# A new written order for the first two batches of a fused attention and expert kernel

## The chip, the cores and the metric

The kernel runs on one core of one Trainium2 chip. The metric is device time in microseconds. Of the kernel before there are three runs: 467.71, 467.88 and 467.96 us, median 467.88 us.

## The reference

Eight batches, eight heads, 576 positions, head size 64, and 32 packed queries a head. In float32:

```
p_packed = softmax(p k^T / 8) v          # 32 rows a head
out      = softmax(q p_packed^T / 8) p_packed
x        = out, heads side by side       # 4608 x 512
h        = max(x w1, x w2, x w3)         # 4608 x 768
result   = h w_out                       # 4608 x 512
```

## The kernel before

The kernel never forms x. Since x = a p_packed with a the second softmax, it multiplies the packed values into the three weights first (the projection, L442, `pw`), and then a with that product (the first layer, L477, `mi`). The second layer (L546, `mo`) uses a seven-product scheme on halves. Operands of the large matmuls are split into a high and a low part, and each product is made of three matmuls: high by high, low by high, high by low.

All work stands in one order that is written out by hand: the table START for batches 0 and 1, the table LOOP for each of the other six. A word of a table names a stage and its indices. Each use of a word runs the stage's generator to its next `yield`, so one word issues some instructions, mostly one to four, on whichever engines they are for. A suffix picks the engine of what this step leaves open: v VectorE, g GpSimd, a ScalarE; without one the default at the line holds. Each engine works through its own list in the order of the words and waits by semaphores. SyncE issues all DMAs in the order of their words as well.

The words that matter here:

- k, v, q, w: loads. w is one of 18 pieces of the first-layer weights (w02 is piece 2 of column block 0) or of 6 pieces of the second-layer weights.
- J10: padding, ten units of 128 columns of matmul on the identity matrix (L144, `idle`), whose result nobody reads.
- S, A, Z, V, K: first attention. S makes the scores (L253), A takes the maximum, the exponential and, for batches 0 and 1, the transposes (L295, L296) and their copies to SBUF; V is the product with the values (L342); K turns the packed result into `pt`.
- Q, B: second attention. Q makes the scores (L370). B is the softmax in groups of 32 (transpose L393, maximum L397, subtraction L399, exponential L401, sum L404, reciprocal L411, multiplication L413, transpose L416) and the split into a high part `a2h` and a low part `a2l` (L133 or L131, and L136).
- C: a weight piece to float32: two ScalarE passes (L189, L194), a shift on VectorE (L203), an addition on GpSimd (L207).
- P: the projection (L442) and its split into `ph` (ScalarE, L453) and `pl` (VectorE, L455). A projection needs all three weight pieces of its column block.
- N, E: the first layer's matmuls, 36 a column block, and the maximum over the three weights: a copy out of PSUM and two maxima (L491).
- X: for batches from 2 on, the spread of the first attention through DRAM instead of transposes on TensorE. W, H, O, F: second-layer operands, the second layer, the sums and the stores.

Scores, transposes and projections share two large PSUM buffers, the first and second layer four small ones. A weight piece keeps its SBUF buffer until GpSimd's addition has read it, and there are six of these. Keys, values, queries and several intermediate tiles share eight buffers more.

Of the kernel before, what the change touches and what calls it, by code (L numbers as in the profile page):

```python
# [37 lines left out]
SCALE = 1.0 / float(D) ** 0.5  # L38

START = """
k00 k01 J10 S0 A01 A01 J7 A01 A00 A00 v01 w00 C00 q010 v00 q000 A01 A00 A00v C00 C00 J1 V00 Z00 q001 V00 V01 Z01
V01 J1 K0 w01 K0v C01 J1 Q0 B010 B010 q011 J1 Q0 C01 k11 k10 C01 B001 B001 B000 B011 B000 B011 w02 B000v B011v  # L50
C00 k21 B010 C01 B010 B010 B000 B000 B000v J11 S1 B011 k20 w12 C02 C02 J12 S2 B001 A10 B001 C02 C02 P00 B010v
A11 A10 A11 B011 B010 B011 C12 B000 P00 B010g Z10 C12 B011 B010 w11 B010v B000g B000 v10 B001 A21 B001v P00 P00
J8 A11 Z11 B001 A20 B001g B011g B000v w10 v11 B000v A21 J1 A10 B001 q10 C12 B001v A20 C10 N00 w21 B011 B010v A10
A11 V101 C10 B011 P00 N00 V101 C11 C11 B001v C11 C12 E000 q11 N00 C21 K1 C21 w20 N00 C10 K1v J1 Q1 E000 E000 C20
C20 C21 w22 Z20 B011 N00 w30 B10 C22 C11 C10 J2 P01 P01 N00 E001 w31 B11 B11 C21 C20 C20 C22 C22 C22 w50 C30 P01
w32 B10 C31 C30 P10 w41 X2 B10v J6 N01 E010 C30 N01 C31 P02 P02 C31 w40 C32 N01 E001 E010 E001 C30 N01 N01 E011
C32 B11 C31 P02 C32 C32 E010 N02 v21 E011 N02 v20 N02 N02 w42 w52 B10 X2 H00 E020 E020 E020 B11 B11 B11v C40 C40
C40 C40 C41 C41 P03 N02 C41 P03 E021v P03 N01 N02 E021 w51 C42 C42 N03 N03 B10 X2 C41 B11 C52 B10 P10 w64 E011
C50 N03 C42 C42 E030v P10 H00 B10 Z21 N03 C52 P04 B11g P11 P04 E031 E021 E030 P04 N03 B10g w62 C52 N03 E030 N04
N04 E031 B11 C51 C51 B10 E040 E031 C52 E040 w65 H00 C50 B11 B11v P11 C51 N04 N04 B10 B10v N04 N04 E041 C64 C64  # L60
E041 E041 E040 C51 N10 C62 H02v E100 N10 N10 C50 C50 V201 q20 P11 P05 H03v w63 H02 C65 C65 C65 N11 E110 C64 C64
H03v C65 N11 N10 E100 V201 K2 E110 P05 C62 W2 N10 P05 E100 E101v C62 w60 H02v C63 N11 E110 H03v K2 q21 Q2 B21
N05 N05 C63 C63 B20 H01 E050 C63 N10 B20 B20 C60 P13 E050 W2 E101 C60 E101 P12 P13 W2 N05 H04v N05 P13 E050 C62
N11 E111 C60 N11 E111 B20 N11 W1v H03v P12 W1 P12 N13 E111 E051 N05 E051 H04 N05 N12 E051 C60 E130 N13 W1 N13
N12 W2 W2v P15 w61 C61 C61 C61 E120v E120 E130 P14 W1 W1v N13 C61 W0v W0v N12 E120 N12 W2 N13 H05g N12 W2 W2 P15
E130 H03 N12 E131 P15 B21 E121 E121 E131 P14 P14 N15 N15 N15 W0 N13 E150 E150 N14 N14 W2 N14 N14 N15 N15 E121
H03v H05 W2 W0 W0v E131 N14 W1 E150 E140 E140 E140 W0 W0 W0 H13 H04v H05 B20 E151v B20 O0 N14 E141v E141 E151
W1v N15 H01v E141 W0 k30 O0 F0 H10 O0 F0 O0 O0 O0 E151 H05v H10 W1 k31 P20 B20 H01 F0 H01v F0 W0v H10v P21 H05
B21v F0 H01 H05v P22 H01v F0 H12 H11 H14v O0 W1g H11v O0 H11v P21 B21 F0 O0 O0 H13 P20 P20 P20 H11v F0 H12 H12v
B20 O0 F0 F0 F0 F0 H13 W1v P20 O0 B20 O0 O0 H14 F0 H14v F0 F0 B21 O1 F0 H15 H15v H15 O1 H11 B21 H13v F1 F1 H15v  # L70
H15 H13v P22 O1 F1 H11v O1 H13v H15v O1 B20 F1 O1 O1 B20 O1 F1 B21 B21g P21 O1 O1 F1 F1 F1 F1 F1 F1 F1 P22 B21
O1 F1 O1 O1 F1 B21 B21 F1 O1 F1
"""


# [11 lines left out]

@with_exitstack
def fused_kernel(ctx: ExitStack, tc: tile.TileContext, kp, qt, va, vb, wi, wo, out):

    nc = tc.nc
# [20 lines left out]
    def on(default):  # L125
        return engine[chosen[0] or default]
# [51 lines left out]
    def convert(j, c):  # L178

        words = staged.pop((j, c)).bitcast(U32).rearrange("p (n two) -> p n two", two=2)
        low, high = words[:, :, 0], words[:, :, 1]
        nc.scalar.activation(  # L189
            out=high.bitcast(F32), in_=high.bitcast(F32), func=AF.Prelu, scale=2.0 ** -111, alpha=-2.0 ** 32,  # L190
        )
# [14 lines left out]
        yield 1
        nc.gpsimd.tensor_tensor(out=dst.bitcast(I32), in0=dst.bitcast(I32), in1=up, op=ALU.add)  # L207
# [3 lines left out]
    def weights(p):  # L211
# [88 lines left out]
        av[b, r] = pa  # L302

    def spread(b):

        x = pool.tile([P, NT, R, NP], F32, name=f"x{b}", tag="b", bufs=NB)  # L310
        first = [sum(len(range(k, NT, 4)) for k in range(c)) for c in range(5)]
        for r in range(R):
            a = a1[b, r][0].rearrange("p (t y) -> p t y", y=NP)
            for c in range(4):
                nc.vector.transpose(out=x[:, first[c]:first[c + 1], r], in_=a[:, c::4])
            yield 1
        kept = dram.tile([4, NP, NT, R, NP], F32, name=f"xk{b}")
        nc.sync.dma_start(out=kept.rearrange("i p t r y -> (i p) (t r y)"), in_=x.rearrange("p t r y -> p (t r y)"))
        at = pool.tile([P, 4, SF + 1, R, NP], F32, name=f"xt{b}", tag="b", bufs=NB)
        for c in range(4):  # L320
            n = first[c + 1] - first[c]
            nc.sync.dma_start(
                out=at[NP * c:NP * c + NP, :, 0:n].rearrange("p i t r y -> p i (t r y)"),
                in_=kept[:, :, first[c]:first[c + 1]].rearrange("i p t r y -> p i (t r y)"),
            )
# [180 lines left out]

    def halves(b, j):

        r = hidden[b, j // 2]
        less = lambda out, x, y: on("g").tensor_tensor(out=out, in0=x, in1=y, op=ALU.subtract)  # L515
# [12 lines left out]
    PRODUCTS = {
# [75 lines left out]
    def weigh_and_turn(b, r):  # L607
# [82 lines left out]
```

## Time and profile before

| | us |
|---|---|
| median of the runs | 467.88 |
| span of the profiled execution | 466.2 |
| time of that execution outside its span | not listed; median less span is 1.7 |
| TensorE busy | 457.3 |
| VectorE busy | 349.8 |
| GpSimd busy | 207.1 |
| ScalarE busy | 172.6 |

The page gives busy shares of the whole span; the views in order of time give a row for each instruction, or for several equal ones, with the time at which it starts, its length, and in brackets how long its engine had been idle and who ended that. Rows of several instructions show their number as x32. The matmuls overlap in TensorE, so a row's length is longer than the distance to the next row.

### The profile page before, as it was taken

The numbers are of one execution on the slowest core, as the hardware profiler recorded it, in microseconds if no ns is written. First come the engines' busy times: TensorE is split into PE (matmuls) and PEld (weight loads), VectorE is DVE, ScalarE is ACT, GpSimd is POOL, SyncE is SP. The second block draws the span as 40 slices with busy tenths as digits, with TensorE's granted clock in tenths as the row PEclk, the third lists the DMA queues.
The fourth block names the chain that finished last, engine by engine and source line by source line (L and its number), as shares of the span: only waits on it lengthen the run. The fifth ranks groups of instructions, "written<-read, shape, count | busy, mean of one in ns | idle before, by whom it ended". The sixth has DMA issues, their size and how long they took to land.

```text
span 466.2 us, 11503 instructions
## 1 busy us (share of the span) xinstructions
PE 457.3 (98%) x4728; PEld 405.3 (87%) x4728; DVE 349.8 (75%) x763; ACT 172.6 (37%) x333; POOL 207.1 (44%) x180
## 2 busy tenths in 40 slices
PE   8899999999999999999999999999999999999996
PEld 3456987998998998989899898989989898998996
DVE  1799989999887677766888678786777678865652
ACT  3486975744332236022340226122350324402330
POOL 0357766756332156503653055612565036531542
PEclk9999999999999999999999999999999999999999
DMA  8999883011127510193104820075101820020002
GB/s 301 403 381 312 315 296 130 1 58 56 57 73 247 192 58 1 49 308 108 59 27 141 257 100 1 27 250 188 59 1 62 296 52 1 27 76 1 2 4 99
DMA packets 25540, 59.20 MB, mean 127 GB/s; under 512 B 2448, under 2 KB 15760, under 8 KB 25488
## 3 DMA queue, kind: packets, MB, share of 16 engines
q1 hardware_dynamic: 25488, 58.47, 36.7%
q8 instruction: 37, 0.61, 0.5%
q14 instruction: 15, 0.12, 0.1%
HBM read 45.48 MB, written 12.98 MB: 125 GB/s over the span
## 4 chain that ended last, share of the span: by engine, by line
PE 92%; DVE 4%; DMA 2%; ACT 0%; issue 0%; POOL 0%; POOLq 0%; ACTq 0%
PE mi L477 49%; PE mo L546 29%; PE pw L442 7%; DMA kt<-in_kp 2%; PE s L253 2%; PE av L342 2%; PE s L370 1%; PE idle L144 1%; DVE mx L266 1%; DVE xt L219 0%; DVE w_sb L203 0%; DVE r L491 0%; ACT a L271 0%; PE tp L342 0%; DVE xl L136 0%
## 5 line engine op out<-in xcount | busy, mean ns | idle before, releaser
L477 PE MATMUL mi<-a2h,ph 128*128 128x288 f32 x576 | 173.9, 302 | 0.7 <-ACT r L131 0.5
L477 PE MATMUL mi<-a2l,ph 128*128 128x288 f32 x576 | 169.7, 295 | 0.0
L477 PE MATMUL mi<-a2h,pl 128*128 128x288 f32 x576 | 169.7, 295 | 0.0
L477 PEld LDWEIGHTS mi<-a2h,ph 128*128 128x128 f32 x576 | 108.1, 188 | 15.5 <-issue 7.1
L477 PEld LDWEIGHTS mi<-a2h,pl 128*128 128x128 f32 x576 | 108.1, 188 | 0.0
L477 PEld LDWEIGHTS mi<-a2l,ph 128*128 128x128 f32 x576 | 108.1, 188 | 0.0
L491 DVE TENSOR_TENSOR r<-mi,r 128x288 f32<-128x288 f32 x192 | 83.3, 449 | 32.6 <-PE mi L477 30.2
L131 ACT COPY r<-mi 128x288 f32<-128x288 f32 x60 | 23.4, 401 | 122.8 <-PE mi L477 122.7
L455 DVE SCALAR_TENSOR_TENSOR pl<-pw,ph 128x768 fp32r<-128x768 f32 (+1 forms) x61 | 46.8, 775 | 4.5 <-ACT ph L453 3.6
L453 ACT ACTIVATE ph<-pw 128x768 fp32r<-128x768 f32 (+1 forms) x61 | 39.9, 675 | 18.8 <-PE pw L442 15.1
L546 PE MATMUL mo<-ych,xl 128*128 128x288 f32 x144 | 42.5, 295 | 0.0
L546 PE MATMUL mo<-ych,xh 128*128 128x288 f32 x144 | 42.4, 295 | 0.0
L546 PE MATMUL mo<-ycl,xh 128*128 128x288 f32 x144 | 42.4, 294 | 0.0
L136 POOL TENSOR_TENSOR yal<-r,yah 128x576 fp32r<-128x576 f32 x13 | 18.6, 1430 | 46.1 <-ACT yah L131 46.1
L271 ACT ACTIVATE a<-s,nm 128x576 f32<-128x576 f32 x16 | 11.9, 741 | 66.8 <-DVE nm L267 60.1
L442 PE MATMUL pw<-w_sb,pt 64*32 64x384 f32 x768 | 36.0, 487 | 0.3 <-POOL w_sb L207 0.3
L207 POOL TENSOR_TENSOR w_sb<-w_sb,wi 128x512 int32<-128x512 int32 x18 | 24.2, 1349 | 26.7 <-DVE z L282 11.8
L515 POOL TENSOR_TENSOR r<-r 128x288 f32<-128x288 f32 (+1 forms) x25 | 27.9, 1128 | 17.5 <-issue 9.0
L133 POOL CAST yah<-r 128x576 fp32r<-128x576 f32 x6 | 4.0, 662 | 57.0 <-DVE r L515 57.0
L546 PE MATMUL mo<-yah,xh 128*128 128x288 f32 x96 | 28.8, 300 | 0.0
L133 DVE COPY r<-mi 128x288 f32<-128x288 f32 x36 | 16.3, 455 | 16.2 <-PE mi L477 16.2
L546 PE MATMUL mo<-ybh,xl 128*128 128x288 f32 x96 | 28.3, 295 | 0.0
(117 smaller groups left out, 885.2 us busy)
## 6 DMA issues: line engine op xcount, KB each, us to landing
kt<-in_kp SPq DMA_DIRECT2D x16, 640.0 KB, 5.2
wi<-in_wi SPq DMA_DIRECT2D x18, 512.0 KB, 6.9
v<-in_va SPq DMA_DIRECT2D x16, 512.0 KB, 5.9
q<-in_qt SPq DMA_DIRECT2D x14, 576.0 KB, 7.1
xk<-x SPq DMA_DIRECT2D x6, 576.0 KB, 4.9
wi<-in_wo SPq DMA_DIRECT2D x6, 512.0 KB, 5.0
out_t<-r SPq DMA_DIRECT2D x8, 288.0 KB, 2.2
out_t<-t SPq DMA_DIRECT2D x8, 288.0 KB, 2.3
```

What stands on the lines that cost most here:

```text
L131: e.copy(out=out, in_=src)
L133: e.tensor_copy(out=out, in_=src)
L136: on(default).tensor_tensor(out=lo, in0=src, in1=hi.bitcast(F32), op=ALU.subtract)
L207: nc.gpsimd.tensor_tensor(out=dst.bitcast(I32), in0=dst.bitcast(I32), in1=up, op=ALU.add)
L271: nc.scalar.activation(out=a.rearrange("p (a b) -> p a b", a=2), in_=s[:, :, 0:HS], func=AF.Exp, bias=nm, scale=SCALE, accum_out=z,)
L442: nc.tensor.matmul(out=ps[r][NP * n:NP * n + NP, 0:NW * P], lhsT=pt_sb[b % 2][o, NP * n:NP * n + NP], rhs=w_sb[o, j, n * NW * P:(n + 1) * ...
L453: nc.scalar.activation(out=hi[:, r], in_=x, func=AF.Copy, scale=2.0 ** -WS)
L455: nc.vector.scalar_tensor_tensor(out=lo[:, r], in0=x, scalar=2.0 ** -WS, in1=hi[:, r].bitcast(F32), op0=ALU.mult, op1=ALU.subtract,)
L477: nc.tensor.matmul(out=sums[b, j, hf, x][:, 0:HS], lhsT=w[:, r, x * P:(x + 1) * P], rhs=a[:, c], start=(r == 0 and n == 0), stop=(r == R - ...
L491: nc.vector.tensor_tensor(out=h, in0=sums[b, j, hf, i][:, 0:HS], in1=h, op=ALU.max)
L515: less = lambda out, x, y: on("g").tensor_tensor(out=out, in0=x, in1=y, op=ALU.subtract)
L546: nc.tensor.matmul(out=ps[:, 0:HS], lhsT=w[:, x, m * P:(m + 1) * P], rhs=h[:, z], start=(p == 0 and i == 0), stop=(p == NQ - 1 and i == 2),)
```

## The change

START is written anew: the order of its words, and with them the order of instructions on all engines and of the DMAs, the lengths of the padding, and the suffixes. LOOP and the functions are the same. Every stage has as many steps as before. The lines of the new file are numbered 26 to 35 lower, since empty lines are gone.

```diff
 START = """
-k00 k01 J10 S0 A01 A01 J7 A01 A00 A00 v01 w00 C00 q010 v00 q000 A01 A00 A00v C00 C00 J1 V00 Z00 q001 V00 V01 Z01
...
+k01 k00 J22 S0 A00 w02 A01 v01 C02 A00 J9 A00 A01 C02 q000 v00 C02 A01 C02 A00v A01v Z00 V00 V00 Z01 w00 V01 C00 V01
...
```

The padding was J10 J7 J1 J1 J1 J1 J11 J12 J8 J1 J1 J2 J6, 62 units, and is J22 J9 J1 J2 J11 J15 J6, 66 units. Over the whole program VectorE has 763 instructions before and 753 now, ScalarE 316 and 313, GpSimd 180 and 193.

TensorE around the transposes of batch 1 (`tp1_0`, `tp1_1` are their results, `idle` is padding, `mi0_0_0_0` the first layer of batch 0). Before:

```order
L144 MATMUL idle15_400<-ident_69 128x512
L144 MATMUL idle16_402<-ident_69 128x512
L295 MATMUL tp1_1_404<-ident_69,a1_1_1_361 128x128 x4
L296 MATMUL tp1_1_404<-ident_69,a1_1_1_361 64x128
L144 MATMUL idle17_432<-ident_69 128x128
L295 MATMUL tp1_0_434<-ident_69,a1_1_0_358 128x128 x4
L296 MATMUL tp1_0_434<-ident_69,a1_1_0_358 64x128
L477 MATMUL mi0_0_0_0_449<-a2h0_0_420,ph0_0_370 128x288
L477 MATMUL mi0_0_0_0_449<-a2h0_0_420,pl0_0_371 128x288
```

And now:

```order
L125 MATMUL idle18_424<-ident_69 128x512
L125 MATMUL idle19_426<-ident_69 128x256
L269 MATMUL tp1_0_428<-ident_69,a1_1_0_341 128x128 x4
L270 MATMUL tp1_0_428<-ident_69,a1_1_0_341 64x128
L269 MATMUL tp1_1_447<-ident_69,a1_1_1_337 128x128 x4
L270 MATMUL tp1_1_447<-ident_69,a1_1_1_337 64x128
L448 MATMUL mi0_0_0_0_469<-a2h0_0_388,ph0_0_421 128x288
L448 MATMUL mi0_0_0_0_469<-a2h0_0_388,pl0_0_422 128x288
```

The two kinds of padding between are one, shorter, and in front of both transposes; behind it the list has no `idle` row until the end.

GpSimd from the first weight piece on (`e0_1` is the softmax tile of batch 0, half 1; `m2` and `z2` its maxima and reciprocal sums; `w_sb` the weights). Before:

```order
L207 TENSOR_TENSOR w_sb_74<-w_sb_74,wi0_0_137 128x512
L399 TENSOR_TENSOR e0_1_232<-e0_1_232,m2_0_1_0_234 128x288
L207 TENSOR_TENSOR w_sb_74<-w_sb_74,wi0_1_217 128x512
L399 TENSOR_TENSOR e0_0_254<-e0_0_254,m2_0_0_288_256 128x288
L207 TENSOR_TENSOR w_sb_74<-w_sb_74,wi0_2_264 128x512
L413 TENSOR_TENSOR e0_1_232<-e0_1_232,z2_0_1_0_274 128x288
L413 TENSOR_TENSOR e0_0_254<-e0_0_254,z2_0_0_0_277 128x288
L413 TENSOR_TENSOR e0_0_254<-e0_0_254,z2_0_0_288_391 128x288
L413 TENSOR_TENSOR e0_1_232<-e0_1_232,z2_0_1_288_364 128x288
L207 TENSOR_TENSOR w_sb_74<-w_sb_74,wi1_2_307 128x512
L136 TENSOR_TENSOR a2l0_1_461<-et0_1_379,a2h0_1_383 128x288
L207 TENSOR_TENSOR w_sb_74<-w_sb_74,wi1_1_381 128x512
```

And now:

```order
L182 TENSOR_TENSOR w_sb_74<-w_sb_74,wi0_2_119 128x512
L370 TENSOR_TENSOR e0_0_241<-e0_0_241,m2_0_0_0_244 128x288
L182 TENSOR_TENSOR w_sb_74<-w_sb_74,wi0_0_197 128x512
L370 TENSOR_TENSOR e0_1_291<-e0_1_291,m2_0_1_0_300 128x288
L370 TENSOR_TENSOR e0_1_291<-e0_1_291,m2_0_1_288_298 128x288
L370 TENSOR_TENSOR e0_0_241<-e0_0_241,m2_0_0_288_305 128x288
L384 TENSOR_TENSOR e0_0_241<-e0_0_241,z2_0_0_0_302 128x288
L384 TENSOR_TENSOR e0_1_291<-e0_1_291,z2_0_1_0_316 128x288
L182 TENSOR_TENSOR w_sb_74<-w_sb_74,wi0_1_261 128x512
L114 CAST a2h0_0_388<-et0_0_350 128x288
L384 TENSOR_TENSOR e0_1_291<-e0_1_291,z2_0_1_288_335 128x288
L117 TENSOR_TENSOR a2l0_0_406<-et0_0_350,a2h0_0_388 128x288
```

Four subtractions stand where two stood, and the high and low parts `a2h`, `a2l` of batch 0 stand between the weight pieces.

VectorE around the split of batch 1's second projection (`pl1_1`). Before:

```order
L491 TENSOR_TENSOR r0_1_773<-mi0_3_1_2_924,r0_1_773 128x288
L491 TENSOR_TENSOR r0_2_953<-mi0_4_0_1_939,r0_2_953 128x288
L136 TENSOR_TENSOR a2l1_1_965<-et1_1_947,a2h1_1_963 128x576
L203 TENSOR_SCALAR w_sb_74<-wi5_1_824 128x512
L136 TENSOR_TENSOR a2l1_0_987<-et1_0_951,a2h1_0_985 128x576
L491 TENSOR_TENSOR r0_2_953<-mi0_4_1_1_989,r0_2_953 128x288
L491 TENSOR_TENSOR r0_2_953<-mi0_4_1_2_996,r0_2_953 128x288
L491 TENSOR_TENSOR r0_2_953<-mi0_4_0_2_971,r0_2_953 128x288
L515 TENSOR_TENSOR r0_1_773<-r0_1_773 128x288
L203 TENSOR_SCALAR w_sb_74<-wi5_0_631 128x512
L455 SCALAR_TENSOR_TENSOR pl1_1_968<-pw1_1_897,ph1_1_967 128x768
L133 CAST ybh0_1_1090<-r0_1_773 128x576
```

And now:

```order
L384 TENSOR_TENSOR e1_0_590<-e1_0_590,z2_1_0_0_850 128x576
L178 TENSOR_SCALAR w_sb_74<-wi5_2_810 128x512
L387 STREAM_TRANSPOSE et1_1_950<-e1_1_604 128x576
L387 STREAM_TRANSPOSE et1_0_953<-e1_0_590 128x576
L462 TENSOR_TENSOR r0_1_758<-mi0_3_1_2_941,r0_1_758 128x288
L178 TENSOR_SCALAR w_sb_74<-wi5_0_724 128x512
L117 TENSOR_TENSOR a2l1_0_976<-et1_0_953,a2h1_0_960 128x576
L462 TENSOR_TENSOR r0_2_958<-mi0_4_0_1_933,r0_2_958 128x288
L462 TENSOR_TENSOR r0_2_958<-mi0_4_1_1_980,r0_2_958 128x288
L462 TENSOR_TENSOR r0_2_958<-mi0_4_0_2_962,r0_2_958 128x288
L426 SCALAR_TENSOR_TENSOR pl1_1_989<-pw1_1_887,ph1_1_988 128x768
L323 TENSOR_SCALAR pp2_1064<-av2_1010,r1_2_0_917 128x64
```

The low part of half 1 (`a2l1_1`) is no longer in this list, and a multiplication of the softmax of batch 1 is.

## Rows read from the trace of the kernel before

**Rows 1.** The page, busy time, share of the span and instructions by engine

```profile
PE 457.3 (98%) x4728; PEld 405.3 (87%) x4728; DVE 349.8 (75%) x763; ACT 172.6 (37%) x333; POOL 207.1 (44%) x180
```

**Rows 2.** Who TensorE waited for from 44 to 460 us: total, times, longest

```profile
PE mi L477 <- ACT r L131: 0.5, 1, 0.5
PE mi L477 <- DVE r L491: 0.2, 1, 0.2
```

**Rows 3.** Stretches: length; busy us of PE, PEld, DVE, ACT, POOL; clock; DMA share; GB/s

```profile
18.00:43.40 25.40, 23.24 (x297) 13.64 (x295) 23.64 (x65) 18.45 (x40) 14.10 (x14) 1.00 1.00 376
43.40:70.00 26.60, 26.60 (x311) 23.61 (x317) 23.73 (x55) 22.38 (x41) 18.21 (x15) 1.00 0.86 297
```

**Rows 4.** TensorE in order of time up to 26 us: start, us, engine, line, operation, idle before

```profile
1.35 4.63 PE L144 MATMUL idle<-ident 128*128 128x512 f32 x6 [1.35 <-POOL ident masks.py:199]
5.92 1.89 PE L253 MATMUL s<-kt 64*32 64x288 f32 x32
...
16.88 2.63 PE L144 MATMUL idle<-ident 128*128 128x512 f32 x6
20.37 1.32 PE L253 MATMUL s<-kt 64*32 64x288 f32 x32 [0.86 <-DMA kt<-in_kp]
...
24.81 1.35 PE L253 MATMUL s<-kt 64*32 64x288 f32 x32 [0.35 <-DMA kt<-in_kp]
25.78 1.03 PE L442 MATMUL pw<-w_sb,pt 64*32 64x384 f32 x16
```

**Rows 5.** TensorE in order of time, 29 to 43.4 us

```profile
29.09 0.66 PE L295 MATMUL tp<-ident,a 128*128 128x128 f32 x4 [0.36 <-ACT a L271]
...
29.69 0.39 PE L144 MATMUL idle<-ident 128*128 128x128 f32 x2
30.35 0.66 PE L295 MATMUL tp<-ident,a 128*128 128x128 f32 x4 [0.27 <-ACT a L271]
...
31.94 1.66 PE L342 MATMUL tp<-v,a1t 128*32 128x64 f32 x80
...
36.24 0.49 PE L144 MATMUL idle<-ident 128*128 128x128 f32 x2
36.66 1.20 PE L370 MATMUL s<-q,pt 64*32 64x288 f32 x32
...
38.68 0.59 PE L144 MATMUL idle<-ident 128*128 128x256 f32 x2
39.56 0.88 PE L442 MATMUL pw<-w_sb,pt 64*32 64x384 f32 x16 [0.29 <-POOL w_sb L207]
...
42.17 1.56 PE L144 MATMUL idle<-ident 128*128 128x512 f32 x4
43.38 0.48 PE L477 MATMUL mi<-a2h,ph 128*128 128x288 f32 x1
```

**Rows 6.** VectorE in order of time, single rows

```profile
7.89 0.76 DVE L266 TENSOR_REDUCE mx<-s 128x1 f32<-128x576 f32 x1 [7.89 <-PE s L253]
...
15.99 0.48 DVE L393 STREAM_TRANSPOSE e<-s 128x288 f32<-128x288 f32 x1 [0.88 <-PE s L370]
...
34.59 0.75 DVE L203 TENSOR_SCALAR w_sb<-wi 128x512 uint32<-128x512 uint32 x2
...
36.59 1.46 DVE L203 TENSOR_SCALAR w_sb<-wi 128x512 uint32<-128x512 uint32 x1
...
68.03 0.95 DVE L455 SCALAR_TENSOR_TENSOR pl<-pw,ph 128x768 fp32r<-128x768 f32 x1
```

**Rows 7.** GpSimd in order of time, one row

```profile
35.14 2.62 POOL L207 TENSOR_TENSOR w_sb<-w_sb,wi 128x512 int32<-128x512 int32 x2 [0.79 <-ACT r L131]
```

**Rows 8.** The page, costliest groups, GpSimd casts: busy, mean ns, idle before

```profile
L133 POOL CAST yah<-r 128x576 fp32r<-128x576 f32 x6 | 4.0, 662 | 57.0 <-DVE r L515 57.0
```

**Rows 9.** ScalarE in order of time, one row

```profile
21.53 0.67 ACT L189 ACTIVATE wi<-wi 128x512 f32<-128x512 f32 x1 [0.67 <-DMA wi<-in_wi]
```

**Rows 10.** TensorE in order of time, one row near 70 us

```profile
69.93 0.51 PE L442 MATMUL pw<-w_sb,pt 64*32 64x384 f32 x1
```

More of the change, by code (lines that the diff above doesn't have):

```diff
@@ L48 @@
 START = """
-k00 k01 J10 S0 A01 A01 J7 A01 A00 A00 v01 w00 C00 q010 v00 q000 A01 A00 A00v C00 C00 J1 V00 Z00 q001 V00 V01 Z01
[L50 to L72, printed above, removed]
+k01 k00 J22 S0 A00 w02 A01 v01 C02 A00 J9 A00 A01 C02 q000 v00 C02 A01 C02 A00v A01v Z00 V00 V00 Z01 w00 V01 C00 V01
+C00 J1 K0 K0v C00 q010 q011 J2 Q0 B000 q001 B000 B000g k10 Q0 k11 B000 w01 k20 J11 S1 C00 B001 B010 k21 B011 w10
@@ new lines @@
+B011 B010 B000 B000a B001 B010g B000 B010 v10 B011g B011 B001g B010 B010a A11 C01 C01 w11 v11 B010 A10 B011 A11
+B000g A10 B010g w12 C01 C01 B011v B000 B001 B011 q10 Z11 B001 B001v J15 S2 B000g B010 C10 B011g A21 A20 q11 w21
+B000g B001 B010a P00 P00 J6 A10 A21 A20 P00 C10 P00 C10 Z10 A11 w22 B010g B011 B001v P00 Z21 A11a A10a N00 B001 w20
+N00 C11 C10 C11 B011a B001g C11 B001g w31 C11 V101 C12 N00 V101 E000a K1 B011g N00 X2 C12 K1a C12 Q1 w32 C21 E000
+B10 C21 C21 w42 C12 N00 B11 w30 E001v w41 P01 P10 E000 w40 C22 C22 C22 w51 P01 P01 v20 C21 N00 C20 C31 E001 C20 C31
@@ new lines @@
+C20 N01 C22 C20 C31 C31 B11 N01 w64 P10 N01 C32 E010v C42 C32 B10 P02 P02 N01 E001 N01 E010 w50 C32 v21 E011a B11v
+B11 N01 C30 P02 C30 C42 N02 N02 E020a E011 C32 C30 C40 E011 X2 E010 N02 C30 P03 N02 C41 C41 N02 B10v C42 P03 C40 C42
+w52 C40 E020 B10 w63 P03 X2 N02 N03 C41 E020 C41 E021a N03 B10 C40 B11 P10 C64 E030a B11v B10a N03 B11 B11g C51 P04
+C51 w61 C51 E021 P04 P11 C50 N03 E030 N03 B10 C52 E030 E031a P04 Z20 E021 C51 N04 C64 C52 E031 B10v N04 C52 N03 w65
+B11 C50 B10 E031 H00g C50 E040a B10a N04 N04 B10v q20 N04 E041a P11 N04 q21 H02g E040 C52 C63 E041 C63 C50 H02a E040
@@ new lines @@
+V201 P05 P11 P05 V201 C64 K2 C61 B11g B11g N11 C65 P05 E041 C64 N11 H00v K2a N10 N05 E100a C65 C63 C65 N10 E100 Q2
+C65 N10 N10 N10 W2g w62 W2g B21 N10 P13 P12 C63 E110v N11 C62 C62 B20 E050a E110 C62 E101a E101 N05 N05 B20 H02v P13
+N05 w60 P13 N05 N11 E110 N13 C60 E050 C61 E100 N13 N11 C60 C62 W2g W2a C60 N05 W1g N11 E051v E101 N13 H00g E050 W2g
+W1v H01a E111a P14 H04v C61 E130a E051 E111 P15 P12 W1v E051 P12 N12 H10g N13 W2a P14 B20g W1a E130 N12 N13 E120a
+C60 C61 E111 E130 W0g W0g H03a W2v P14 N13 H03v H04a E120 E131a H01v B20 N12 N14 N14 E131 E131 N12 W0v W2g E140v N14
@@ new lines @@
+P15 H10a H01g P22 P21 P15 W2g N15 W0a N14 H01v N14 W1v N12 H04g E140 N15 H03g N12 E121a N15 N15 H01a k30 W2g W0v N15
+E150a E141v H05a W1a E120 B20 W0a E121 H05g H05g H05g E140 P21 E151a B21 N14 E150 E141 W1v W0v E121 E151 B20a H03v
+H05a N15 E150 P22 H05v O0 B21v H13a O0 H11v W0g k31 E151 O0 W1v H03a F0 O0 H03v H12g E141 H01v O0 F0 H10v O0 O0 O0
+O0 W1a F0 B20 H11v H12a W1g H14g F0 F0 H12v H11g W0g O0 O0 H14a O0 F0 F0 H11g W0g H14g O0 F0 F0 F0 F0 F0 B21 F0 F0
+H11a O0 B21 B21a P21 H11v O1 H13v H13v H15a F1 B21 F0 H15v O1 O1 H13v H15g O1 H15v F1 O1 F1 H13a H15v O1 H13v F1
@@ L73 @@
+H15v F1 B20v F1 F0 O1 O1 B21v B21 O1 O1 B21g F1 B21g F1 F1 O1 B20 O1 O1 P22 O1 F1 F1 F1 F1 P20 P20 F1 F1 F1 P20 B20g
+P20 P20 B20g
 """
```

## The prediction

> **What bounds the kernel now.** I read the busy shares first, then who TensorE waits for, then TensorE in order of time through the first 45 us. TensorE is busy for 98% of the span [rows 1]. From 44 to 460 us it waits twice, for 0.7 us in all [rows 2], so from there on the time is its list of matmuls, which the change leaves as long as it was. What can move lies before 44 us, and it is of two kinds: padding (the matmuls on the identity, L144) and waits. The reader is to see the alternation of the two in [rows 4, 5]: padding, then mostly a short wait, then work. The DMA share is 1.00 from 18 to 43.4 us, and VectorE is busy for 23.6 of these 25.4 us and 23.7 of the next 26.6 [rows 3]. So two things stand just behind TensorE: the stream of inputs, and VectorE.
>
> The sum is made against the profiled execution: its span is 466.2 us, and I take 1.7 us to lie around it, the difference to the median of the runs, 467.88 us.
>
> **The padding that goes.** After the transposes of the second batch begin at 29.09, padding and its waits take 29.69 to 30.35, 36.24 to 36.66, 38.68 to 39.56 and 42.17 to 43.38 [rows 5]: 0.66 + 0.42 + 0.88 + 1.21 = 3.17 us. The new list has no padding after this point. If it gets there no later and never waits, it gains 3.17 us: the upper bound of this part. If the data that the padding covered is no earlier, the same time comes back as waits: the lower bound is no gain.
>
> **The longer padding at the start.** J10 becomes J22. Ten units took 4.63 us, and by 16.88 eleven units take 2.63 us [rows 4]: 0.46 and 0.24 us a unit, the engine at half and at full tempo. The first scores (32 matmuls) took 1.89 us, the second 1.32 us, so the tempo rose inside the first, near 7 us. I put 13 units before that point and 9 behind it: the scores start at 9.0 instead of 5.92 (at most 1.35 + 22 x 0.46 = 11.5) and, at full tempo, take 1.35 us. VectorE's first maximum moves from 7.89 [rows 6] to 10.4: 2.5 us late. The first transpose of the softmax of batch 0 comes at 17.8 instead of 15.99, because two paddings between go and the rest is the same list; bounds 17.0 and 18.5.
>
> What hides this: the next scores waited 0.86 us for the keys at 20.37, and the third set 0.35 us at 24.81 [rows 4]. The bytes ordered up to these keys are the same in sum, so they arrive at the same times. Padding J11 (2.6 us) behind the queries fills TensorE to 20.4, J15 (3.2 to 3.6) behind the second scores to about 24.8. The head's delay is gone for TensorE there. It costs nothing as long as the keys come no earlier, and at most 2.5 us if the softmax chain shows it later.
>
> **The softmax of batch 0.** Its subtractions, high parts and low parts go from VectorE to GpSimd. The third weight piece lands at 21.5 as before [rows 9], and its shift on VectorE stands behind the two maxima of the second scores (0.76 each): 24.6. With 0.4 for the shift and 1.31 for GpSimd's addition [rows 6, 7] the first projection starts at 26.4, against 25.78 [rows 4]: 0.6 late. The padding behind it is J6 instead of J8, 0.5 less; the rest is the same, so the transposes start at about 28.7 against 29.09: 0.4 ahead. Twelve matmuls of the first layer now stand in front of the product with the values, where six stood. That product waits for ScalarE's copies as before, and I leave it at 31.95; TensorE has done six matmuls (0.8 us) more by then. Behind it 0.42 + 0.88 + 1.21 = 2.51 us of padding are gone. Projections of the second piece start when VectorE has read both halves of the new scores, which adds a wait of 0.7 us. Then the second piece's first-layer matmul, at 43.38 before, comes at 43.38 - 0.8 - 2.51 + 0.7 = 40.8: **2.6 us ahead**.
>
> GpSimd's high part of 288 columns isn't in the trace. The nearest row is its 0.66 for 576 columns [rows 8]; half of it is the lower bound, all of it the upper, and I take 0.4. Two stand in this chain, so they can cost 0.5 us more, and the data they make is used 1 us or more after my times for it.
>
> **What is given back.** From 43 to 65 us I followed the weight pieces: landing, two passes on ScalarE, a shift on VectorE, an addition on GpSimd, the projection. In the new order the third, fourth and fifth projection of batch 0 find their last piece 0.1, 0 and 0.2 us late: 0.3 us together; bounds 0 and 1.5. The spread attention of the third batch lands some 0.5 us before its use: nothing, with 1 us at risk.
>
> The term that matters is the sixth projection. It reuses the PSUM buffer of the second batch's second projection, whose last reader is a subtraction on VectorE, 68.03 to 68.98 in the trace [rows 6]; the projection started at 69.93 [rows 10]. In the new order 18 first-layer matmuls (2.4 us) that stood before it stand behind it, and with the gain above TensorE would be there at 64.9. VectorE's list up to that subtraction shrinks from 136 to 128 instructions only, and began 1.8 to 2.5 us later. I get its end at 65.5 to 67; I take 65.8. TensorE waits 1.0 us; bounds 0 and 2.2.
>
> Behind this point VectorE's list in the first two batches is lighter by some ten instructions in all, GpSimd's heavier by 13, and all first-layer matmuls of batch 1 stand before the second layer of batch 0, so I price this stretch at 0, with 0.5 us at risk at its end, where GpSimd makes the last low part of batch 2 just ahead of its use.
>
> Sum: 2.6 - 0.3 - 1.0 = 1.3 us. 466.2 - 1.3 + 1.7 = **466.6 us**.
>
> **A rule against the change.** A shift on VectorE takes 0.38 (two in 0.75), but 1.46 at 36.59, when GpSimd was in the second of two additions that began at 35.14 and took 2.62 us, to 37.76 [rows 6, 7]: it ended 0.3 us after GpSimd did. So VectorE's shift waits for GpSimd's instruction. My walk has four such waits before 65 us, 0.3 to 0.8 each, 2 us in all; without them the sixth projection would not wait and the sum would be the first rival's.
> The Trainium skill, "SBUF — State Buffer", section "Who interferes with whom", says that VectorE in a two-port mode, or with two SBUF inputs, and GpSimd lock each other out for a whole instruction. By that rule, the trace agrees, every instruction moved to GpSimd is also a risk for VectorE.
>
> **Rivals.**
> - *VectorE keeps up.* Its idle and blocked time shrinks with GpSimd taking the softmax, the sixth projection doesn't wait: 466.2 - 2.6 + 1.7 = 465.3, or 464.7 with the whole 3.17. For it: two subtractions and four low parts leave its list early. Against it: 23.6 of 25.4 us busy.
> - *Nothing comes of it.* The stream of inputs is full until 43 us and orders the same bytes, so the weights allow no more than before, and padding returns as waits: 467.9, or 467.4 to 468.3. For it: the DMA share of 1.00. Against it: in the trace the second-piece projection waited for GpSimd (0.29), not for DMA.
> - *Slower: VectorE blocked by GpSimd.* In 18 to 70 us GpSimd was busy for 32.3 us [rows 3]; it gets about 5 us more, in which 18 shifts and six two-input instructions of VectorE fall. One blocked shift costs 1.46 - 0.38 = 1.1 us. From three more blocked ones than I counted ahead of the sixth projection, the gain and the 0.9 us that can be told are gone; with four to five (5 us), less 2 us that VectorE idles anyway, TensorE waits 3 us more: 469.6. For it: [rows 6]. Against it: shifts mostly stand just behind an addition that waits for them.
> - *The head's delay survives*: TensorE reaches the second scores 1 to 2 us after their keys, and the forecast loses 1.5: 468.1.
>
> **How the numbers follow.** Forecast (465.9 to 467.3) 0.45, VectorE keeps up 0.18, nothing or a surviving delay 0.21, slower 0.16. A change under 0.2% (0.94 us) can't be told from none by this measurement. Faster by more: 0.36 of the forecast's 0.45 and the 0.18, 0.54. Within: the other 0.09, and 0.20 of the 0.21: 0.29. Slower: 0.17. The range, 465.0 to 468.8, leaves out the end of the slower case and of the best.
>
> **What would show it.** The first scores at 9.0 and at full tempo; second and third scores at 20.4 and 24.8, still released by DMA; the first projection at 26.4, released by GpSimd; no TensorE gap above 0.8 us between 28 and 43 us, and the second piece's first layer at 40.8. Then a wait of TensorE at the sixth projection at 65 to 67 us, released by VectorE's subtraction, and hardly any behind it. The forecast is wrong if the second scores start later than 21, if the 40.8 comes past 42.5, or if TensorE waits more than 3 us between 43 and 142 us.

## The result, and the profile after

The changed kernel takes 470.44 us (median of 4 runs, 469.83 to 472.12) against 467.92 us (467.71 to 468.53, 4 runs) for the kernel before: 1.0056 times, 95% interval 1.0036 to 1.0075. It is slower by 0.56%, where 466.6 us was forecast and the range ended at 468.8.

Up to 60 us the profile after runs much as forecast. TensorE in order of time, from the view to which [rows 4, 5] belong:

```profile
1.36 6.48 PE L125 MATMUL idle<-ident 128*128 128x512 f32 x12 [1.36 <-POOL ident masks.py:199]
7.77 1.20 PE L227 MATMUL s<-kt 64*32 64x288 f32 x32
...
20.14 1.17 PE L227 MATMUL s<-kt 64*32 64x288 f32 x24 [0.21 <-DMA kt<-in_kp]
...
24.66 1.20 PE L227 MATMUL s<-kt 64*32 64x288 f32 x32
25.65 0.85 PE L413 MATMUL pw<-w_sb,pt 64*32 64x384 f32 x16
...
31.32 1.46 PE L313 MATMUL tp<-v,a1t 128*32 128x64 f32 x80
...
37.72 1.53 PE L413 MATMUL pw<-w_sb,pt 64*32 64x384 f32 x32 [0.83 <-DVE e L364]
40.87 0.40 PE L448 MATMUL mi<-a2h,pl 128*128 128x288 f32 x1 [0.50 <-DVE pl L426]
```

The last 24 matmuls of the second scores wait 0.2 us for their keys, at 20.14; the third scores start at 24.66 straight behind the padding, without a wait (20.37 and 24.81 before, both behind a wait). A new wait of 0.83 stands at 37.72, and the second piece's first layer is at 40.87, where 40.8 was forecast. The 145th matmul of the first layer starts at 58.94, before at 61.52: 2.6 us ahead, with the same work done up to it.

Then most of the loss comes in one place. Whom TensorE waited for, over the whole span (total, times, longest), and the row of the third batch's product with the values, after and before:

```profile
PE av L313 <- DMA xt<-xk: 4.0, 1, 4.0
...
PE mi L448 <- DVE r L462: 0.8, 1, 0.8
PE pw L413 <- DVE e L364: 0.8, 1, 0.8
```

```profile
68.00 1.38 PE L313 MATMUL av<-v,xt 128*32 128x64 f32 x73 [4.03 <-DMA xt<-xk]
```

```profile
68.76 1.38 PE L342 MATMUL av<-v,xt 128*32 128x64 f32 x73
```

In the kernel before this product waited for nothing; [rows 2] has 0.7 us of waits in all. SyncE's queue says why its data are late. First of before, then of after (start, length of the issue, what is issued; `xk` is the store of the spread attention, `xt` its four loads):

```profile
47.12 3.71 SPq L154 DMA_DIRECT2D wi<-in_wi  x3
50.93 0.38 SPq L318 DMA_DIRECT2D xk<-x  x1
57.60 2.78 SPq L322 DMA_DIRECT2D xt<-xk  x4
```

```profile
51.34 0.33 SPq L135 DMA_DIRECT2D wi<-in_wi  x1
53.68 0.33 SPq L135 DMA_DIRECT2D wi<-in_wo  x1
54.06 0.42 SPq L289 DMA_DIRECT2D xk<-x  x1
62.48 1.76 SPq L293 DMA_DIRECT2D xt<-xk  x4
```

The store is issued 3.1 us later, behind a second-layer piece (`in_wo`, w63) whose own issue had to wait 1.9 us for a buffer that GpSimd frees. From issue to complete landing it takes 8.4 us where it took 6.6, and the last load lands at 67.9 where it landed at 64.0. TensorE meanwhile comes to the product at 64, 4.8 us earlier than before: 2.4 are left of its head start, and 2.4 come from 18 matmuls that now stand behind the product and stood ahead of it.

The later issue belongs to the new order, the long way of the store to this execution: in the profiles of e1_fill, e3_late and e4_head below, with the DMAs in the same order, the store is issued at 53.6 to 54.7 and takes 6.6 to 7.0 us, and the last load lands at 65.4 to 66.9.

The wait costs a second time. Stretches of the profile after (length; busy us of TensorE, its weight loads, VectorE, ScalarE, GpSimd; granted clock; DMA share; GB/s):

```profile
64.00:68.00 4.00, 0.01 (x1) 0.04 (x2) 1.16 (x2) 1.10 (x2) 2.38 (x3) 1.00 0.93 264
68.00:69.00 1.00, 1.00 (x64) 0.93 (x64) 0.00 (x0) 0.00 (x0) 0.00 (x0) 1.00 1.00 401
69.00:70.00 1.00, 1.00 (x39) 0.47 (x32) 0.41 (x3) 0.00 (x0) 0.00 (x0) 0.63 1.03 420
...
71.00:72.00 1.00, 1.00 (x6) 1.00 (x6) 0.18 (x1) 1.00 (x2) 0.83 (x1) 0.50 1.12 446
72.00:73.00 1.00, 1.00 (x7) 1.00 (x7) 1.00 (x2) 1.00 (x3) 0.00 (x0) 0.67 0.94 383
```

After 4 us of idling the granted clock falls to 0.50, the level of 1.2 GHz, from about 69.3 to 72.7 us, and in these 3.4 us TensorE does the work of 1.7. This is the slowest of the four executions, 472.12 us at a mean clock of 0.995. One more has 0.995, and takes 470.41; the other two have 1.000 and take 469.83 and 470.46. So an execution with the fallen clock can be 1.7 us shorter than this one. A shorter wait would explain it, but only this execution was profiled; the sums below are this profile's and not the median's.

One more wait of 0.8 us stands near 90 us, for VectorE. Its rows before that:

```profile
86.52 1.00 DVE L194 TENSOR_TENSOR xt<-xt,xb 128x256 f32<-128x256 f32 x1
87.44 1.06 DVE L482 TENSOR_TENSOR r<-r 128x288 f32<-128x288 f32 x1
88.42 1.38 DVE L178 TENSOR_SCALAR xb<-wi 128x512 uint32<-128x512 uint32 x1
89.72 0.81 DVE L462 TENSOR_TENSOR r<-mi,r 128x288 f32<-128x288 f32 x2
```

And GpSimd's beside them:

```profile
84.84 2.40 POOL L117 TENSOR_TENSOR xl<-xb,xh 128x1024 fp32r<-128x1024 f32 x1 [0.20 <-ACT xh L112]
87.20 0.99 POOL L482 TENSOR_TENSOR r<-r 128x288 f32<-128x288 f32 x1
88.14 1.37 POOL L370 TENSOR_TENSOR e<-e,m 128x576 f32<-128x576 f32 x1
```

TensorE waits for the first of the two maxima in VectorE's last row. Each of the three instructions ahead of them ends 0.3 us after a GpSimd instruction: at 87.52 after 87.24, at 88.50 after 88.19, at 89.80 after 89.51. The subtraction (L482) takes 1.06 us, and 0.45 in the 31 other places of this trace; the shift takes 1.38, and 0.38 alone [rows 6]. So this wait is the one that the forecast's rival had in mind, VectorE blocked by GpSimd.

The sum of the profile: -2.6 + 4.0 + 1.7, and 0.6 more at 90 us (1.0 between two matmuls there, against 0.4 in before's gap of that kind at 95 us), is +3.7; the spans differ by 470.3 - 466.2 = 4.1, so 0.4 us are spread over smaller gaps.

### The profile page after: what moved, and what is told of

Its sections match the earlier page's. It is cut to its first block, busy times and chain, and to the rows that moved or that the text cites. A ratio compares the mean times of both kernels' runs of the same rounds, so it can differ in the third digit from the quotient of the medians.

```text
span 470.3 us, 11498 instructions
## 1 busy us (share of the span) xinstructions
PE 458.0 (97%) x4724; PEld 405.9 (86%) x4724; DVE 345.6 (73%) x753; ACT 170.4 (36%) x330; POOL 217.1 (46%) x193
## 4 chain that ended last, share of the span: by engine, by line
PE 89%; DMA 7%; DVE 2%; ACT 1%; issue 1%; POOL 0%; SPq 0%; POOLq 0%; ACTq 0%
PE mi L448 46%; PE mo L511 29%; PE pw L413 7%; PE idle L125 2%; DMA wi<-in_wi 2%; DMA kt<-in_kp 2%; PE s L227 2%; PE av L313 2%; DMA xk<-x 2%; PE s L341 1%; DMA xt<-xk 1%; ACT ph L424 0%; DVE mx L240 0%; DVE pl L426 0%; POOL w_sb L182 0%
## 5 line engine op out<-in xcount | busy, mean ns | idle before, releaser
L462 DVE TENSOR_TENSOR r<-mi,r 128x288 f32<-128x288 f32 x192 | 83.6, 448 | 33.1 <-PE mi L448 29.4
L117 POOL TENSOR_TENSOR yal<-r,yah 128x576 fp32r<-128x576 f32 x15 | 21.6, 1439 | 46.6 <-ACT yah L112 46.5
L482 POOL TENSOR_TENSOR r<-r 128x288 f32<-128x288 f32 (+1 forms) x30 | 34.8, 1170 | 17.6 <-issue 9.0
L511 PE MATMUL mo<-ybl,xh 128*128 128x288 f32 x96 | 28.3, 295 | 0.0
```

Source lines behind the costliest of these rows:

```text
L117: on(default).tensor_tensor(out=lo, in0=src, in1=hi.bitcast(F32), op=ALU.subtract)
L462: nc.vector.tensor_tensor(out=h, in0=sums[b, j, hf, i][:, 0:HS], in1=h, op=ALU.max)
L511: nc.tensor.matmul(out=ps[:, 0:HS], lhsT=w[:, x, m * P:(m + 1) * P], rhs=h[:, z], start=(p == 0 and i == 0), stop=(p == NQ - 1 and i == 2),)
```

## The experiments

Theory 1: the loss is TensorE's wait for the spread attention's DMA, with the clock behind it. Rival: VectorE, locked out by GpSimd, sets the pace, and the DMA only happened to end last. All are compared with the kernel before on the same chip.

**e1_fill.** Padding in the place of the wait.

```diff
-V201 P05 P11 P05 V201 C64 K2
+J17 V201 P05 P11 P05 V201 C64 K2
```

> The changed kernel with 17 units of padding on TensorE (about 4.1 us at full clock) put just ahead of the third batch's product with the values, so that TensorE is busy while it would wait; nothing else moves. Theory 1 (the loss is TensorE's 4.0 us wait at that product for the spread attention's DMA, and the half clock that followed it for 3.4 us): the product still starts at about 68.0, the granted clock stays at full level from 68 to 73 us, and what comes behind is 1.7 us earlier than in the profile of the changed kernel: span 468.6 us, time 470.4. Rival (VectorE, locked out by GpSimd, is the true bound there, and the DMA only ended last): VectorE's later steps stay where they were, and the span stays at 470.3 within 0.5.

470.27 us (1.0042, 1.0030 to 1.0054), span 468.5. Its stretch behind the product:

```profile
68.00:72.00 4.00, 4.00 (x98) 3.23 (x87) 2.13 (x6) 2.09 (x4) 1.32 (x1) 1.00 1.03 413
```

The clock stays at 1.00, and the span is 1.8 us under that of the changed kernel's profile, as theory 1 had it. Of these, 0.5 us are a product that starts earlier, at 67.54 with the padding's end (its data had landed at 66.3 in this run); the other 1.3 are about the clock, which the stretches above put at 1.7. The median, 2.2 us over the kernel before, is hardly under the changed kernel's 2.5: the filling keeps the clock up but takes no wait away, and two of the four executions of the changed kernel had no fall to save.

**e2_store.** The load w63 behind the store instead of ahead of it.

```diff
-w52 C40 E020 B10 w63 P03 X2 N02
+w52 C40 E020 B10 P03 X2 w63 N02
```

> The changed kernel with one SyncE load moved: the second-layer weight piece w63, which had to wait for GpSimd's additions and stood ahead of the store of the third batch's spread attention, stands behind the store and its four loads. Theory 1 (TensorE waits at the third batch's product with the values because the spread attention is stored too late): the store is issued at 51.7 instead of 54.1 us, the last of its loads lands at 65.0 to 65.5 instead of 67.9, TensorE's wait falls from 4.0 to 1.3 to 1.8 us, the clock does not fall, and the time is 466.1 to 468.5 us. Rival (VectorE locked out by GpSimd): the wait named DMA goes, one of the same length on VectorE's subtraction or GpSimd's low part takes its place, and the time stays at 470 us.

469.40 us (467.89 to 470.11, 11 runs; 1.0025, 1.0016 to 1.0034); the profiled run 468.33. SyncE and TensorE:

```profile
51.65 0.43 SPq L289 DMA_DIRECT2D xk<-x  x1
58.55 1.75 SPq L293 DMA_DIRECT2D xt<-xk  x4
```

```profile
63.85 1.46 PE L313 MATMUL av<-v,xt 128*32 128x64 f32 x80
...
73.93 0.40 PE L448 MATMUL mi<-a2h,ph 128*128 128x288 f32 x1 [0.73 <-ACT r L112]
...
86.42 0.40 PE L448 MATMUL mi<-a2h,ph 128*128 128x288 f32 x1 [0.84 <-DVE r L462]
```

In the profiled run the wait is gone. The last load lands at 63.65 instead of 67.90: 2.4 us of that are the earlier issue, and 1.8 a quicker store and quicker loads in this execution, so not every execution is rid of the wait (e5_copy's profile, with the DMAs in this order, has 1.3 us of it). The time falls by 1 us in the median and not by 2 to 4: from 2.5 us over the kernel before to 1.3. Two waits of 0.9 and 1.0 us (between the matmuls) stand behind the product now, for a ScalarE copy behind a second-layer piece that landed at 72.3, and for VectorE. From the 145th first-layer matmul to the end the profile without the DMA wait still loses 3.0 us against the kernel before. So the rival is right in part: waits for other engines take back some of what the DMA's gives.

**e3_late.** The product behind the sixth projection and twelve first-layer matmuls.

```diff
-V201 P05 P11 P05 V201 C64 K2 C61 B11g B11g N11 C65 P05 E041 C64 N11 H00v K2a
+P05 P11 P05 C64 C61 B11g B11g N11 C65 P05 E041 C64 N11 V201 V201 K2 H00v K2a
```

> The changed kernel with the third batch's product with the values moved behind the second batch's sixth-projection step and twelve first-layer matmuls (the sixth projection of batch 0 comes first and takes the PSUM buffer that is free earlier); all other work keeps its order. Theory 1: TensorE starts the sixth projection at 63.7 to 64.2 without a wait, then waits 1 to 2 us for the low part on GpSimd that ended at 66.46, and comes to the product at 67.5 to 68.5, when its data land: the 4.0 us wait turns into 1 to 2 us, and the time is 466.5 to 468.5 us. Rival (VectorE locked out by GpSimd bounds this stretch): about the same 4 us of waits come on VectorE's or GpSimd's halves, and the time stays at 470 us.

471.33 us (1.0060, 1.0046 to 1.0075): a miss. The wait for the DMA is gone; in its place stands the longest of the waits that are left, and VectorE's row:

```profile
PE av L328 <- DVE pp L323: 2.1, 1, 2.1
```

```profile
68.69 0.43 DVE L178 TENSOR_SCALAR xb<-wi 128x512 uint32<-128x512 uint32 x1 [3.98 <-PE av L313]
```

A shift now stands ahead of the scaling of the product (L323), and it had to wait for that very product to end; VectorE idled 4 us before it. The move itself made this wait, so it speaks for neither theory. The granted clock was 0.52 from 72 to 74 us here, behind a wait of 2.1 us, and the mean clock is 0.995 or 0.996 in four of the six executions; the two at 1.000 took 469.73 and 469.96 us.

**e4_head.** The padding at the start as before.

```diff
-k01 k00 J22 S0
+k01 k00 J10 S0
```

> The changed kernel with the padding at the start cut from 22 units to the 10 of the kernel before. Theory 1: the head is hidden behind the keys that land at 20.1 and 24.7 us; the second and third scores start within 0.3 us of the changed kernel's, the wait at the third batch's product stays at 4 us, and the time is 470.4 us within 0.7. Rival (the 2.5 us by which the longer padding delays the softmax of batch 0 survive in VectorE's list): VectorE's list is 1.5 to 2.5 us earlier up to 65 us and the time falls by 1 to 2.5 us.

471.84 us (1.0072, 1.0057 to 1.0088). The second and third scores start at 19.37 and 24.50 in its profile, as theory 1 had it; the product waits 2.4 us for the DMA and not 4. Nothing is gained by the shorter head: the rival falls. The median is 0.7 above what theory 1 allowed, and in four of six runs the mean clock is 0.995 or 0.996.

**e5_copy, e6_max, e7_all.** On top of e2_store, one more edit each.

```diff
 e5: -E110v N11 C62 C62 B20 E050a E110 C62 E101a E101
     +E110v N11 B20 E050a E110 E101a C62 C62 C62 E101
 e6: -W1v H01a E111a P14 H04v C61 E130a E051 E111 P15 P12 W1v
     +H01a E111a P14 E130a E051 E111 W1v H04v C61 P15 P12 W1v
 e7: -V201 P05 P11 P05 V201
     +P05 V201 P11 P05 V201
```

> The kernel of run e2_store (the store of the spread attention ahead of the load w63) with one more move: on ScalarE the two passes over the weight piece w62 stand behind two copies of first-layer sums instead of ahead of them. In e2_store's profile TensorE waited 0.9 us at 73.9 for such a copy, which stood behind the first pass, whose piece landed at 72.3. Theory 1 (with the DMA wait gone, what is left of the loss is waits for engines that stand behind second-layer weights now): the wait at 73.9 falls to 0.2 or less, the one of 1.0 at 86.4 stays, and the median falls from 469.4 to 468.5 to 468.9. Rival (the waits are interchangeable and VectorE sets the pace): the 0.9 us come back in the next 20 us as a longer wait for VectorE, and the median stays at 469.4.

> The kernel of e5_copy with one more move: on VectorE two maxima of first-layer sums stand ahead of three instructions for later use (a combination of second-layer weights, a half of the hidden layer, a shift of a weight piece), behind which they stood. In e2_store's profile TensorE waited 1.0 us at 86.4 for the first of these maxima (85.92 to 86.38), behind 3.3 us of those three. Theory 1: that wait goes too, and the median is 467.5 to 468.2, the time of the kernel before. Rival (VectorE sets the pace): the three instructions are late for their own use, a wait of 0.5 to 1 us appears between 88 and 110 us, and the median stays above 468.4.

> The kernel of e6_max with the sixth projection of batch 0 ahead of the third batch's product with the values on TensorE, as filling, with nothing moved on VectorE; the product then needs the spread attention at about 65.1 instead of 63.6 us. Theory 1: in the executions in which the DMA still held the product in e2_store (its median stood 1.1 us above its profiled run) the wait goes, for 0.5 us at the projection's weights; the median is 466.5 to 467.8, below the kernel before. Rival (VectorE sets the pace): no change against e6_max within 0.4 us.

Medians 468.69 (1.0013, 1.0004 to 1.0022), 468.57 (1.0012, 1.0004 to 1.0021) and 468.44 us (1.0008, 1.0000 to 1.0017). e5's median lies where theory 1 put it. Its profile, taken in the slowest of its twelve runs (470.06), has the DMA wait back with 1.3 us, since the store took from 51.29 to 60.34; the wait for ScalarE at 73.9 is gone, and one of 1.3 us for VectorE stands at 71.3, as the rival had it. In e6 the wait at 86.4 went and came back as 0.8 us at 90.1, as the rival had it, and the median is above 468.4. e7 is within 0.4 of e6, the rival's number, and did not beat the kernel before. The steps from e5 to e7 are smaller than their intervals; what the four moves together do is clear, from 2.5 us over the kernel before to 0.3. The chain of waits of e7 (start, length, what) runs through VectorE:

```profile
85.76 0.21 DVE r L462
85.96 0.17 issue
86.13 1.06 DVE xt L194
87.19 0.18 DVE r L482
87.37 0.11 issue
87.48 0.41 DVE xb L178
87.90 0.34 DVE xb L194
88.23 0.37 DVE r L462
88.60 0.88 DVE pl L426
89.48 0.14 issue
89.61 0.88 PE pw L413 x16
```

The instructions that e6 moved back now hold the subtraction of a projection (`pl`), and TensorE waits 0.8 us for it at 89.6. e7 is still 2.5 us ahead at the 145th first-layer matmul (59.06) and 0.8 us behind at the last second-layer ones (462.77 against 461.96). At the 260th, with the same work done in both kernels, it is 0.4 ahead: 2.0 of the 3.3 us go before 82 us, where TensorE waits 0.5 us for GpSimd at 64.6 and 0.6 for VectorE at 67.5, and the rest mostly between 87 and 98 us.

**e8_mirror.** The kernel before, with its store behind three second-layer pieces.

```diff
-N03 B10 X2 C41 B11 C52 ... C52 E040 w65 H00
+N03 B10 C41 B11 C52 ... C52 E040 w65 X2 H00
```

> The kernel before with one thing of the changed kernel's: the store of the third batch's spread attention and its loads stand behind three second-layer weight pieces (w64, w62, w65) on SyncE, as the changed kernel has one ahead. In the trace of before the loads end at 64.0 and the product starts at 68.8: a slack of 4.7 us. Theory 1: the loads end 4 us later for the three pieces' transfer (1.4 us each) and as much again as these must wait for GpSimd to free their buffers; by what goes beyond 4.7 us TensorE waits at that product: 1 to 4 us, and the time rises by as much, to 469 to 472 us, with half clock behind the wait where it is over 3 us. Rival (VectorE, locked out, bounds the stretch): the product's place is paid for by VectorE's later list, no such wait shows, and the time stays within 0.5 of 468.0.

469.89 us (1.0050, 1.0037 to 1.0063).

```profile
54.17 3.93 SPq L154 DMA_DIRECT2D wi<-in_wo  x3
58.15 0.42 SPq L318 DMA_DIRECT2D xk<-x  x1
```

```profile
69.58 1.38 PE L342 MATMUL av<-v,xt 128*32 128x64 f32 x73 [0.88 <-DMA xt<-xk]
```

The last load lands at 69.39, 5.4 us later; less the slack of 4.8 that is 0.6, and TensorE waits 0.88, just under the forecast 1 to 4. The profiled run, the fastest of the five, is 1.2 us over before's span, the median 1.8 over before's. So the place of the store alone makes the old kernel slower in the same way. The 3 us that the expectation sets for half clock are shown by no run: in e3_late and e4_head the clock fell behind waits of 2.1 and 2.4 us.

**e9_nopad.** The kernel before without the paddings of [rows 5].

```diff
-w10 v11 B000v A21 J1 A10 ... K1v J1 Q1 ... C10 J2 P01 ... B10v J6 N01
+w10 v11 B000v A21 A10 ... K1v Q1 ... C10 P01 ... B10v N01
```

> The kernel before without its last four paddings (those at 29.7, 36.2, 38.7 and 42.2 us of its trace, 3.17 us with their waits); nothing else changes, apart from the PSUM buffers that the padding no longer takes. It tests the first term of the forecast alone. Theory 1 (the padding covered nothing that could not come earlier; it was the changed order that gave the head start away again): TensorE comes to the second piece's first layer 1 to 2.5 us earlier than 43.38 and the time falls by 0.5 to 2 us, to 466.1 to 467.6. Rival (the padding stood where data came late, and VectorE sets the pace of the stretch up to 100 us): the 3 us come back as waits for VectorE, ScalarE and GpSimd, part of them before 44 us and the rest before 100 us, and the time stays at 468.1 within 0.5.

466.92 us (466.68 to 467.21, 9 runs; 0.9977, 0.9967 to 0.9987): faster than both kernels.

```profile
30.12 0.65 PE L295 MATMUL tp<-ident,a 128*128 128x128 f32 x4 [0.49 <-ACT a L271]
...
39.35 0.88 PE L442 MATMUL pw<-w_sb,pt 64*32 64x384 f32 x16 [0.84 <-POOL w_sb L207]
```

Of the 3.17 us 1.75 came back at once, part of it as longer waits for ScalarE and GpSimd. The 37th first-layer matmul comes at 41.96, 1.42 us ahead of 43.38, and 1.34 us are still there at the last second-layer matmuls (460.61). This is what theory 1 said.

**e10_early, e12_cover.** On top of e7_all: two VectorE instructions earlier; in e12 also six matmuls behind the product.

```diff
 e10: -N05 W1g N11 E051v E101 N13
      +N05 W1g N11 H04v C61 E051v E101 N13
 e12: -P05 V201 P11 P05 V201 C64 K2 C61 B11g B11g N11 C65
      +P05 V201 P11 P05 V201 B11g B11g N11 C64 K2 C61 C65
```

> The kernel of e7_all with two instructions of VectorE (a half of the hidden layer and a shift of a weight piece, 1.5 us) moved from its full stretch at 87 us into a stretch at 80 us in which its profile shows it idle for 2 of 5 us. In e7_all's profile the chain of waits from 85.7 to 96.4 us runs along VectorE, and TensorE waits 0.8 us at 89.6 for a subtraction of a projection and 0.4 at 96.4 for a maximum. Theory 2 (with the DMA wait gone, the order of VectorE's list between 85 and 97 us is what holds TensorE): both waits shrink, by 0.6 to 1.2 us in all, and the median is 467.3 to 467.9. Rival (the waits are set by the dates at which the first-layer sums are done, not by the list): the waits stay and the median stays at 468.4 within 0.3.

> The kernel of e10_early with six first-layer matmuls (0.8 us) put between the third batch's product with the values and the transpose that has to wait for VectorE's scaling of that product: in e7_all's profile TensorE waited 0.6 us there. Theory: that wait goes if the low part that these matmuls need is there by 66.5 us, and the median falls by 0.3 to 0.6 us against e10_early, to 466.9 to 467.5; with it the kernel would beat the one before by 0.6 us or more. Rival (waits are interchangeable): no change against e10_early within 0.2.

471.69 us (1.0067, 1.0055 to 1.0079) and 470.67 (1.0061, 1.0049 to 1.0074): both missed. VectorE and GpSimd in e10:

```profile
80.60 2.62 DVE L482 TENSOR_TENSOR r<-r 128x288 f32<-128x288 f32 x1
```

```profile
80.34 2.57 POOL L117 TENSOR_TENSOR xl<-xb,xh 128x1024 fp32r<-128x1024 f32 x1
```

The same subtraction took 0.45 in e7_all, with GpSimd idle, and 1.06 in the kernel after. It began just after a long low part on GpSimd, ended 0.3 us after it, and TensorE waited 2.3 us for the copy behind it. Here the lock of the forecast's slower rival is seen at its price: 2.2 us. e12_cover has the same 2.62 and the same wait of 2.3; its median is 1.0 us under e10_early's, but their executions overlap (470.26 to 472.20 and 470.28 to 471.81).

**e11_dve.** e7_all with the softmax of batch 0 on the engines of before (the suffixes of its four generators; one is shown).

```diff
-B000 ..g..a.g.gg
+B000 ..v..v.g.vv
```

> The kernel of e7_all with the softmax of batch 0 on the engines of the kernel before: two subtractions, three casts, three low parts and two small additions more on VectorE, fewer on GpSimd. It tests the forecast's slower rival, that each instruction given to GpSimd blocks VectorE. If the engines' choice is the cost: VectorE is blocked less often, and the median falls by 0.5 to 2 us, to 466.4 to 467.9. If VectorE is simply the fuller engine: its list before 35 us grows by some 4 us, less what it idled, the first matmuls of the first layer start 0.5 to 2 us later, and the median rises by 0.5 to 2 us, to 469 to 470.4.

470.16 us (1.0046, 1.0034 to 1.0058), 1.7 us over e7_all. The first layer of batch 0 waits 1.2 us for VectorE at 32.4, and the first layer's 37th matmul comes at 41.12 instead of 40.34. In this order of the words, giving this softmax to GpSimd was a gain, which speaks against the forecast's slower rival.

## Why the prediction was wrong

The step that failed: "The spread attention of the third batch lands some 0.5 us before its use: nothing, with 1 us at risk." In the profile it landed 3.9 us after TensorE had come for it. Of the 3.9 us by which the last load came later than before, 3.1 are the store's later issue and 1.8 its longer way in this execution, less 1.0 that the loads were quicker; TensorE came 4.8 us earlier, and the slack had been 4.8. The prediction shows its working for the weight pieces, and none for the store's place in SyncE's queue. Its own sign of being wrong came true here: TensorE waited more than 3 us between 43 and 142 us. e2_store takes the wait away by moving one load, e8_mirror gives one of the same kind to the old kernel.

This step is not the whole miss. Against the kernel before, the forecast was -1.3 us, the changed kernel has +2.5 and e2_store +1.3 in the medians. So the store's place is worth 1.2 of the 3.8 us there; the larger part, 2.6 us in e2_store and still 1.6 in e7_all, is the second failure below.

- *2.6 us ahead at 43 us*: right, and e9_nopad shows that half of it can be kept to the end when the rest of the order is left alone.
- *The longer head*: hidden, as worked out, and e4_head agrees. When the clock rises is luck: with the same head it rose to full at 4.4 us in this profile, and the first scores came at 7.77 and not 9.0; in e1_fill and e2_store it rose at 7.5 us, and they came at 9.30 and 9.35, close to the forecast. There the third scores start at 25.3 to 25.4, 0.7 us after the changed kernel's, yet the 145th first-layer matmul stands at 58.9 in all three.
- *The softmax on GpSimd*: the first projection came at 25.65 without a wait, where 26.4 was forecast (26.3 to 26.4 in e1_fill and e2_store, with the later head). Priced at nothing to 0.5 us of cost; e11_dve shows 1.7 us of gain.
- *The sixth projection waits 1.0 us*, "the term that matters": not seen. VectorE's subtraction ended at 65.17, 0.6 before the forecast, and the product's wait covers it; in e2_store, without that wait, TensorE does not wait there either.
- *"I price this stretch at 0, with 0.5 us at risk at its end"* (behind the sixth projection): the second failure. That behind 44 us the time is TensorE's list of matmuls held for the old order, and not for the new one. From the 145th first-layer matmul to the end TensorE loses 1.0 us in the changed kernel beside the DMA's wait and the clock, 3.0 us in e2_store and 3.3 in e7_all. VectorE's list is lighter: from 65 to 100 us it is busy for 33.1 us in the kernel before and for 27.4 in e7_all. But a lighter list is no earlier one where each entry waits for an input or stands behind another that does; that this is the reason here was not tested.
- *The clock*: in no term. 1.3 to 1.7 us in the profiled run, none in those at 1.000.
- *Slower: VectorE blocked by GpSimd*, 469.6: nearest in time, not in cause. It needed four to five more blocked instructions ahead of the sixth projection than the four that the walk had counted. From 18 to 65 us three of VectorE's instructions outlast the shortest of their kind by some 0.2 us or more, 1.3 us in all, and in the kernel before three as well, 2.4 us in all. Behind 65 us the lock is in the trace after (1.38 us for a shift of 0.38) and in e10_early (2.62 for 0.45), but it is the smaller part. The Trainium skill, "SBUF — State Buffer", section "Who interferes with whom", says that a VectorE instruction with two inputs in SBUF contends with a GpSimd instruction that reads SBUF, and that the port pair between them is an exclusive lock; e10's two rows agree.

What stays open: which of the moves behind 59 us takes e7_all's head start. From 85 us on the chain names VectorE's list, but most of the head start is gone before that, and no version of the order without the waits was found.

## What to carry to other kernels

When a change brings an engine to a point earlier, list every input of that point with its slack, transfers first, and follow the transfer's issue through its own queue: here one load ahead of a store, and a buffer that the load waits for, cost 1.2 us in the medians and 5.7 in the worst profile, where taking out the padding alone won 1.1. Take out padding by itself before the order is written anew; the simple edit won 1.1 us and the large one lost 2.5. A long wait of TensorE can have a second price in the clock, 1.7 us here. And where a wait is taken away, expect part of it to come back at other engines.

## What the runs showed of the hardware

- A store of 576 KB landed at its first engine at 58.61 and at its last at 62.43, with 15 GB/s moved from 60.0 to 62.5 us; in the kernel before the two lay 0.8 us apart. The loads that read it back wait for the last. With the DMAs in one order the store took 6.8 us in e2_store's profile, 7.8 in e6_max's and 9.0 in e5_copy's. This may be why e2_store's runs spread over 2.2 us, and those of before over 1.3; that was not tested.
- The granted clock fell to 0.50 some 0.8 to 1.3 us after the end of a wait of TensorE: of 4.0 us in the changed kernel, 2.4 in e4_head, 2.3 in e12_cover and 2.1 in e3_late. It did not fall behind e10_early's wait of 2.3 in its profile.
- VectorE's subtraction of 288 columns took 2.62 us beside a GpSimd subtraction of 2.57, and 0.45 without one.
